# Two rows of wo loaded by the lower eight DMA engines alone, with O turned to match

## The chip, the cores and the metric

One core of one Trainium2 chip. The metric is device time of one execution in microseconds (us); each kernel ran several times, and medians, lowest and highest are quoted. The trace holds one execution of each kernel; the other executions give a time, a span (first to last instruction) and a mean granted clock only.

## The reference, cut to what matters

A decode step of attention plus an MLP, both on the normalised input, with 8 batch rows, 32 heads, 4096 keys of 128:

```python
q = (x @ wq).reshape(B, Sq, H, Dh).transpose(0, 2, 1, 3)
p = softmax(einsum("bhqd,bhkd->bhqk", q, k_cache) * Dh ** -0.5)
o = einsum("bhqk,bhkd->bhqd", p, v_cache)
A = o.transpose(0, 2, 1, 3).reshape(B, Sq, H * Dh) @ wo       # wo: 4096 x 576
h = gelu(einsum("bsd,df->bsf", layernorm(x), w1) + b1)
return x0 + A + einsum("bsf,fd->bsd", h, w2) + b2             # w2: 4608 x 576
```

The caches are 537 MB. The weights wo and w2 (10.0 MB together) are loaded last.

## The kernel before

The large operands are all streamed by SyncE's queue, in order: wq, w1, then keys and values of 32 tiles, then w2 and wo. wo is viewed as 128 partitions of 32 rows: partition `p` holds rows `32p` to `32p+31` of the matrix. A product takes one such "row" `r` of all partitions against `OT[:, r, :]`.

```python
CUTS = (0, 12, 23, 30, RO)                     # RO = 32: four loads of wo
...
sy.wait_ge(sem["kf"], NX * (NT - 1) + 2)
sy.dma_start(out=w2_sb..., in_=w2_v).then_inc(w2_in, 16)
for n, (r0, r1) in enumerate(zip(CUTS, CUTS[1:])):
    if n == 1:
        sy.wait_ge(sem["kf"], NX * (NT - 1) + 5)
    wo_in.append(nc.alloc_semaphore(f"in_wo{n}"))
    to, rows = wo_rows(r0, r1), wo_v[:, r0 * D:r1 * D]
    sy.dma_start(out=to, in_=rows).then_inc(wo_in[-1], 16)
...
# TensorE, after the last tile
te.wait_ge(w2_in, 16)
hidden_part()                                  # 36 matmuls on w2, first half
te.wait_ge(sem["on"], NT)
for b in range(B):                             # turn O: 8 matmuls into S_ps[0]
    ...
hidden_part()                                  # 36 matmuls on w2, second half
te.wait_ge(sem["on"], NT + 1)                  # VectorE has copied S_ps[0] to OT
for n, (r0, r1) in enumerate(zip(CUTS, CUTS[1:])):
    te.wait_ge(wo_in[n], 16)
    for r in range(r0, r1):                    # two matmuls a row
        ins = accumulate(te, OT[:, r, :], rows[:, r - r0, :], stop=(r == RO - 1))
```

The softmax here doesn't subtract the row's maximum and nothing guards it: scores larger than these inputs give would overflow.

## Time and profile before

| | before |
|---|---|
| time, median of the first three runs | 1292.88 us (1292.85 to 1292.97) |
| span of the traced run | 1291.5 us |
| memory stream over the span | 431 GB/s |
| w2 landed | 1277.83 us |
| TensorE's last matmul ends | 1289.56 us |

The profile's chain of waits of the kernel before; columns: start, length, what.

```profile
1248.87 4.03 PE s_ps L651 x9
...
1252.92 24.91 DMA ring<-in_B_w_dram
1277.83 0.04 issue
1277.87 4.49 PE acc L377 x36
1282.36 0.54 PE s_ps L701 x8
1282.90 6.68 PE acc L377 x100
1289.58 0.03 issue
1289.60 0.45 DVE fin L604
```

Read it from the bottom: the final cast waits for TensorE, TensorE works without a break from 1277.87 on, and what released it there is w2's load. The last loads of wo don't appear, so each had landed before TensorE asked for it.

The timeline of TensorE's matmuls in the last 18 us, kernel before; columns: start, length, engine, line, operation, result and sources, how many, and the idle time before it with its releaser.

```profile
1277.87 4.49 PE L377 MATMUL acc<-ring,hT_sb 128*8 128x288 bf16 x36 [2.77 <-DMA ring<-in_B_w_dram]
1282.29 0.61 PE L701 MATMUL s_ps<-low,Ox 128*128 128x32 bf16 x8
1282.83 2.81 PE L377 MATMUL acc<-ring,hT_sb 128*8 128x288 bf16 x36
1285.47 4.09 PE L377 MATMUL acc<-ring,OT 128*8 128x288 bf16 x64
```

The same 36 matmuls take 4.49 us the first time and 2.81 us the second: the granted clock, the share of full speed that TensorE is given, was 0.5 from 1276.94 to 1283.77 and full after it.

The trace also records sixteen landing increments for each of these loads, as many as the profile counts DMA engines; they are read here as one for each engine. Fourteen of w2's fall between 1275.99 and 1276.95, and the last two at 1277.80 and 1277.83. A 16 KB instruction packet passed at 29.99 us and another at 75.88 us (1.02 and 1.03 us). Of the later cache loads' sixteen increments, one came 1.1 us after the others from the first packet on, and two from the second on. So two engines, called the late ones here, each took one packet and stayed behind to the end.

### The profile page before, as it was taken

To read this page: it belongs to the slowest core of one execution; us is meant where nothing else is said; L and a number is where in the kernel's file an instruction comes from. 1 tells how busy PE (TensorE), PEld (TensorE's weight loads), DVE (VectorE), ACT (ScalarE), POOL (GpSimd) and SP (SyncE) were. 2 spreads that over 40 slices of the span, in tenths; PEclk is the share of its full clock that TensorE was granted. 3 is DMA by queue.
4 is the path that set the end of the run, shared out by engine and by line. 5 is a ranking of instruction groups with operands and counts; after the bars stand their busy time and mean duration, and the time that the engine had idled before them with its cause. 6 is when DMAs were issued, how large, how long until landed. Compare 5 with 4: busy or idle time off the path is not lost. (4 is left out here: it accounts for less than half of the span.)

```text
span 1291.5 us, 14664 instructions
## 1 busy us (share of the span) xinstructions
PE 734.5 (57%) x4707; PEld 321.8 (25%) x4707; DVE 829.2 (64%) x740; ACT 56.7 (4%) x181; POOL 2.4 (0%) x12
## 2 busy tenths in 40 slices
PE   4654565554565554565554565554566554565557
PEld 1222232222222222222222232222222222222223
DVE  2655677655677655677655677655677655577654
ACT  2000000000000000000000000000000000000000
POOL 0000000000000000000000000000000000000000
PEclk8778887778887777887777887778887777888778
DMA  9999999999999999999999999999999999999998
GB/s 421 440 425 436 436 426 447 426 426 449 424 426 451 422 428 449 422 430 447 422 438 438 426 436 436 426 445 428 426 447 426 426 449 424 426 451 422 430 447 348
DMA packets 10409, 557.00 MB, mean 431 GB/s; under 512 B 1163, under 2 KB 1188, under 8 KB 1446
## 3 DMA queue, kind: packets, MB, share of 16 engines
q1 hardware_dynamic: 10368, 556.93, 99.7%
q8 instruction: 2, 0.03, 0.0%
q10 hardware_dynamic: 38, 0.02, 0.0%
q14 instruction: 1, 0.01, 0.0%
HBM read 556.94 MB, written 0.01 MB: 431 GB/s over the span
## 5 line engine op out<-in xcount | busy, mean ns | idle before, releaser
L651 PE MATMUL s_ps<-ring,ident 128*128 x2048 | 541.1, 421 | 517.4 <-PEq L649 516.9
L559 DVE TENSOR_TENSOR ring<-ring,qb 128x4096 bf16<-128x4096 bf16 x256 | 578.9, 2282 | 281.8 <-DMA ring<-in_A_k_cache_dram 281.5
L651 PEld LDWEIGHTS s_ps<-ring,ident 128*128 128x128 bf16 x2048 | 216.4, 106 | 829.3 <-issue 678.7
L534 DVE TENSOR_REDUCE sc<-s_ps 128x32 f32<-128x512 f32 x256 | 171.3, 682 | 0.0
L670 PE MATMUL o_ps<-ring,ebd 128*32 128x512 bf16 x2048 | 116.4, 380 | 0.0
L546 DVE TENSOR_TENSOR ebd<-es,head 128x1536 bf16<-128x1536 bf16 x64 | 77.8, 1216 | 0.0
L569 DVE RECIPROCAL rec<-tot_ps 128x8 f32<-128x8 f32 x32 | 6.6, 207 | 110.8 <-PE oT_ps L678 110.8
L582 ACT ACTIVATE es<-sc 128x192 bf16<-128x192 f32 x64 | 19.8, 310 | 1104.2 <-DVE sc L534 1104.2
L670 PEld LDWEIGHTS o_ps<-ring,ebd 128*32 128x32 bf16 x2048 | 51.6, 97 | 62.6 <-issue 13.6
L678 PE MATMUL oT_ps<-selc,ob 128*128 128x8 f32 x256 | 33.9, 259 | 12.3 <-ACT ob L586 12.3
L678 PEld LDWEIGHTS oT_ps<-selc,ob 128*128 128x128 f32 x256 | 31.0, 191 | 15.2 <-ACT ob L586 15.2
L586 ACT ACTIVATE ob<-o_ps 128x512 f32<-128x512 f32 x32 | 19.1, 597 | 80.3 <-PE o_ps L670 80.3
L428 DVE TENSOR_SCALAR ring<-ring 96x384 f32<-96x384 f32 x2 | 0.7, 352 | 26.5 <-ACT ring L427 26.5
L545 DVE TENSOR_TENSOR Es<-Ep 128x1 f32<-128x1 f32 x32 | 5.1, 160 | 13.3 <-ACT es L582 13.3
L674 PEld LDWEIGHTS tot_ps<-headf,Es 128*128 128x128 f32 x64 | 9.5, 187 | 13.6 <-issue 13.6
L674 PE MATMUL tot_ps<-headf,Es 128*128 128x8 f32 x64 | 12.4, 266 | 0.0
L582 ACT ACTIVATION_READ_ACCUMULATOR es<-sc 128x1 f32 x64 | 11.9, 186 | 0.0
L417 PE MATMUL o_ps<-ring 128*32 128x384 bf16 x27 | 7.9, 861 | 2.9 <-DMA ring<-in_B_w_dram 2.9
L574 DVE TENSOR_TENSOR Ox<-on,quad 128x32 bf16 x32 | 6.2, 192 | 4.8
L377 PE MATMUL acc<-ring,hT_sb 128*8 128x288 bf16 x72 | 7.3, 381 | 2.8 <-DMA ring<-in_B_w_dram 2.8
L417 PE MATMUL s_ps<-ring 128*32 128x384 bf16 x27 | 7.9, 863 | 0.0
L339 PE MATMUL tot_ps<-ident,ring 40*128 40x16 bf16 x9 | 0.7, 206 | 11.6 <-DVE ring L317 11.6
(76 smaller groups left out, 61.5 us busy)
## 6 DMA issues: line engine op xcount, KB each, us to landing
ring<-in_B_w_dram SPq DMA_DIRECT2D x2, 5184.0 KB, 25.2
ring<-in_A_wq_dram SPq DMA_DIRECT2D x1, 4608.0 KB, 13.7
ring<-in_A_wo_dram SPq DMA_DIRECT2D x1, 1728.0 KB, 28.6
ring<-in_A_wo_dram SPq DMA_DIRECT2D x1, 1584.0 KB, 26.5
ring<-in_A_wo_dram SPq DMA_DIRECT2D x1, 1008.0 KB, 28.5
ring<-in_A_k_cache_dram SPq DMA_DIRECT2D x32, 31.9
ring<-in_A_v_cache_dram SPq DMA_DIRECT2D x32, 30.5
ring<-in_A_wo_dram SPq DMA_DIRECT2D x1, 288.0 KB, 28.7
```

Of the source, the lines that this page charges most:

```text
L377: i = e.matmul(acc[m][m * OP:m * OP + B, :ND], lhsT=lhsT, rhs=rhs[:, m * ND:(m + 1) * ND], start=start, stop=stop)
L417: i = e.matmul(h_ps[j][s * MP:(s + 1) * MP], lhsT=lhsT, rhs=wv[:, r0:r0 + HK, :], **flags)
L534: ins = ve.tensor_reduce(out=sc[:, n * CB:(n + 1) * CB], in_=bank_of(x).rearrange("p (c d) -> p c d", d=DL), axis=AX.X, op=ALU.add)
L546: ve.tensor_tensor(out=ebd[:, ja:jb], in0=es[:, a:b].rearrange("p (j c) -> p j c", c=4).unsqueeze(2) .to_broadcast([P, nj, G, 4]), in1=hea ...
L559: ve.tensor_tensor(out=k, in0=k, in1=qb[:, bass.ds(t, 1), :].to_broadcast([P, CB, Dh]), op=ALU.mult,).then_inc(sem["prod"], 1)
L569: ve.reciprocal(out=rec[:], in_=tot_ps[:, :G]).then_inc(sem["rec"], 1)
L582: sa.activation(out=es[:, a * CB:b * CB], in_=sc[:, a * CB:b * CB], func=ACT.Exp, scale=scale, accum_out=Ep[:, i:i + 1]).then_inc(sem["x"], 1)
L586: sa.activation(out=ob[:].rearrange("r c d -> r (c d)"), in_=o_ps, func=ACT.Copy).then_inc(sem["ob"], 1)
L651: ins = te.matmul(to, lhsT=idn, rhs=k[:, :, d * DL:(d + 1) * DL], start=(d == 0), stop=(d == Dh // DL - 1))
L670: ins = te.matmul(o_ps[m * MP:(m + 1) * MP, :], lhsT=ebd[:, j].rearrange("p g c -> p (g c)"), rhs=vals[:, c:c + 4, :], start=(j < M), stop ...
L674: te.matmul(tot_ps[:, :G], lhsT=Es[:].to_broadcast([P, P]), rhs=headf[:], start=True, stop=True).then_inc(sem["vf"], 1)
L678: ins = te.matmul(oT_ps[:, :G], lhsT=ob[:, c, :], rhs=selc[:, c, :], start=(c == 0), stop=(c == 3))
```

## The change

The intent is to take work from the two late engines. The eight engines that carry the new loads are called the lower eight here, the other eight the upper. Packet records carry no engine number; followed from packet to packet, neither late one carried a packet of the eight-row x load (eight landing increments in the trace of before). That the new loads run on the same eight engines as the x load, and so without the late ones, was the assumption; no trace had shown it. The change takes rows 0 and 1 of wo (288 KB) out of the ordinary load and has the lower eight carry them alone, in four loads of 32 partitions, whose source counts to eight in its outermost dimension. That count puts the rows on partitions in another order, so TensorE turns O's two rows to match.

```diff
-    CUTS = (0, 12, 23, 30, RO)
+    SHIFT = 2
+    CUTS = (0, SHIFT, 12, 23, 30, RO)
...
+    act(["ident"], ["turned"], lambda e: e.activation(
+        func=ACT.Copy, out=turned[:].rearrange("p (q e j) -> p q e j", e=NE, j=NJ),   # NE, NJ = 8, 4
+        in_=idn.rearrange("p (q j e) -> p q e j", e=NE, j=NJ)))
...
-        sy.dma_start(out=to, in_=rows).then_inc(wo_in[-1], 16)
+        if r1 > SHIFT:
+            sy.dma_start(out=to, in_=rows).then_inc(wo_in[-1], 16)
+            continue
+        st, w = RO * D, (r1 - r0) * D
+        for q in range(0, P, NE * NJ):
+            in_ = rows[q:q + 1]
+            sy.dma_start(
+                out=to[q:q + NE * NJ],
+                in_=bass.AP(in_.tensor, in_.offset, [[st, NE], [NE * st, NJ], [1, w]])
+            ).then_inc(wo_in[-1], 16)
...  # VectorE
     ve.wait_ge(sem["end"], 2)
+    ve.tensor_copy(
+        out=OT[:, :SHIFT], in_=S_ps[1][:, :SHIFT * B].rearrange("p (r b) -> p r b", b=B)
+    ).then_inc(sem["on"], 1)
+    ve.wait_ge(sem["end"], 3)
...  # TensorE
-    for n, (r0, r1) in enumerate(zip(CUTS, CUTS[1:])):
-        te.wait_ge(wo_in[n], 16)
+    te.matmul(
+        S_ps[1][:, :SHIFT * B], lhsT=turned[:], rhs=OT[:, :SHIFT].rearrange("p r b -> p (r b)"),
+        start=True, stop=True).then_inc(sem["end"], 1)
+    for n in (1, 0, *range(2, len(wo_in))):
+        r0, r1 = CUTS[n], CUTS[n + 1]
+        if not n:
+            te.wait_ge(sem["on"], NT + 2)
+        te.wait_ge(wo_in[n], 16 if n else 16 * P // (NE * NJ))
```

The four loads stand in the queue right behind w2 and ahead of the rest of wo.

More of the change, by code (lines that the diff above doesn't have):

```diff
@@ L181, in decode @@
     OT = sb("OT", [P, RO, B], BF16)
+    NE, NJ = 8, 4
+    turned = sb("turned", [P, P], BF16)
     hT_sb = sb("hT_sb", [P, R, 2 * B], BF16)
@@ L452, in decode @@
     mlp_done = [od.last(e) for e in ("tensor", "vector", "scalar")]
-    CUTS = (0, 12, 23, 30, RO)
+    SHIFT = 2
+    CUTS = (0, SHIFT, 12, 23, 30, RO)
+    HOMES = 12
     W2_AT = home(NT, 0)
     WO_AT = (W2_AT + 2 * R * D, home(NT - 1, 0))
-    assert WO_AT[0] + CUTS[1] * D <= WO_AT[1] and (RO - CUTS[1]) * D <= 3 * BLOCK
+    assert WO_AT[0] + HOMES * D <= WO_AT[1] and (RO - HOMES) * D <= 3 * BLOCK
     w2_sb = ring[:, W2_AT:WO_AT[0]].rearrange("p (v r d) -> p v r d", v=2, d=D)
     def wo_rows(r0, r1):
-        at = WO_AT[0] + r0 * D if r0 < CUTS[1] else WO_AT[1] + (r0 - CUTS[1]) * D
+        at = WO_AT[0] + r0 * D if r0 < HOMES else WO_AT[1] + (r0 - HOMES) * D
         return ring[:, at:at + (r1 - r0) * D]
@@ L480, in decode @@
     for n, (r0, r1) in enumerate(zip(CUTS, CUTS[1:])):
-        if n == 1:
+        if r0 == HOMES:
             sy.wait_ge(sem["kf"], NX * (NT - 1) + 5)
@@ L603, in decode @@
     ve.wait_ge(sem["end"], 2)
+    ve.tensor_copy(
+        out=OT[:, :SHIFT], in_=S_ps[1][:, :SHIFT * B].rearrange("p (r b) -> p r b", b=B)
+    ).then_inc(sem["on"], 1)
+    ve.wait_ge(sem["end"], 3)
     ve.tensor_copy(out=fin[:B], in_=acc[0][:B, :ND]).then_inc(fin_d, 1)
-    sa.wait_ge(sem["end"], 2)
+    sa.wait_ge(sem["end"], 3)
     sa.activation(
```

## The prediction

> **What bounds the kernel now.** The memory stream: the slices show a DMA share of 9 tenths nearly throughout, 431 GB/s over 1291.5 us. The change acts on the last 15 us. There the chain of waits ends: w2's load lands at 1277.83; then TensorE runs without a gap to 1289.58 (36 matmuls of the hidden part 4.49 us at half clock, 8 that turn O 0.54 us, 36 + 64 on `acc` 6.68 us); then the casts and two stores.
>
> **What is late in the stream.** The trace records sixteen landing increments for each load. After about 85 us fourteen of them fall within 1 us, the last two about 1.1 us later (last wo load: 1287.06 to 1288.00, then 1288.84 and 1288.88). By the packets, the two late ones each took one 16 KB instruction packet (at 29.99 and 75.88 us, 1.02 us each) and never caught up. Neither carried packets of the eight-row x load[...].
>
> **What the change moves.** wo's rows 0 and 1 are 288 KB, 18 KB per engine. The upper eight lose 18 KB: 0.68 us at the 27.2 GB/s of a 64 KB packet (2.41 us). The lower eight gain sixteen 2,304-byte packets of 94 ns and have eight packets shortened: +0.83 us (estimate). So the last landing should come at 1288.4 to 1288.6 instead of 1288.88, set now by the lower engines.
>
> **How much is critical.** Next to nothing. In the wo part TensorE takes 61.3 ns per `acc` matmul (starts 122.5 ns apart per row) and shows no gap. Row 12 starts at 1286.94, its load landed at 1285.75; row 23 at 1288.29, landed 1288.17; row 30 at 1289.15, landed 1288.88. Every load is there, by 0.12 us at the closest. What starts TensorE is w2, issued ahead of the shifted rows; its landing stays at 1277.8.
>
> **What the change adds.** On TensorE's critical run: one 128x128 weight load and a matmul of 16 columns. The eight like it took 67 ns each at half clock, plus about 0.14 us to change over; at full clock I estimate 0.05 to 0.15 us. VectorE's copy of the turned rows (0.2 to 0.4 us) hides behind the 20 matmuls of rows 2 to 11 (1.2 us). Three more issues on SP come 20 us ahead of need; the extra ScalarE copy falls in an idle stretch before 17.7 us.
>
> **Prediction.** Before 1292.88; after 1292.95 us, 8 in 10 between 1292.5 and 1293.4. Faster by over 2%: 0.005; within 2%: 0.99; slower by over 2%: 0.005.
>
> **What would show it.** Right: w2 still lands near 1277.8; the last landing is 0.3 to 0.5 us earlier, and no two engines stand 1.1 us behind in the last wo loads; TensorE runs gapless from w2 to its end, near 1289.65. Wrong: gaps in the wo part; TensorE waiting for rows 0 and 1; the new loads on sixteen engines.
>
> **What would make it wrong.** The granted clock returns to full at 1283.77; it may do so elsewhere in unprofiled runs, and with a faster TensorE the last landing would bind, giving back up to 0.4 us. The added instructions may move an instruction packet to another time or engine, which moves w2's landing by up to 1.1 us either way.

The sum is 1292.88 us plus the turn, estimated at 0.05 to 0.15 us.

## More of the kernel before

Sums over three stretches of the kernel before (a packet is counted where it starts, so a DMA share can pass 1); columns: stretch, its length, busy time of PE, PEld, DVE, ACT, POOL, granted clock, DMA share, GB/s.

```profile
core 0: us, PE busy (x) PEld busy (x) DVE busy (x) ACT busy (x) POOL busy (x), PEclk, DMA share, GB/s
1275.60:1276.80 1.20, 0.00 (x0) 0.00 (x0) 0.19 (x1) 0.00 (x0) 0.00 (x0) 1.00 1.02 432
1276.80:1278.20 1.40, 0.33 (x4) 0.23 (x6) 0.00 (x0) 0.00 (x0) 0.00 (x0) 0.55 0.98 415
1278.20:1280.00 1.80, 1.80 (x20) 0.94 (x16) 0.00 (x0) 0.00 (x0) 0.00 (x0) 0.50 0.99 419
```

The stream is even here.

## The result, and the profile after

| | before | after |
|---|---|---|
| time, median of 6 runs | 1292.86 us (1292.79 to 1292.97) | 1294.28 us (1293.27 to 1295.38) |
| time and span of the traced run | 1293.01, 1291.5 us | 1293.60, 1292.0 us |
| w2 landed, last two engines | 1277.80, 1277.83 us | 1278.52, 1278.73 us |
| w2 landed, the other fourteen | 1275.99 to 1276.95 us | 1276.02 to 1276.61 us |
| last landing of wo | 1288.88 us | 1289.09 us |
| clock returns to full | 1283.77 us | 1283.17 us |

The ratio of the times is 1.0011 (95% interval 0.9998 to 1.0024). Ratios here are the mean time of one kernel's fast runs over that of the other's of the same rounds, so not quite the ratio of the medians quoted. The median lies 1.4 us above and the runs spread over 2.1 us instead of 0.2.

The rows did move: of the ordinary load of rows 2 to 11, six engines landed at 1280.25 to 1280.85 and ten at 1281.80 to 1282.20, as fits six upper engines with less to carry, eight lower ones with more, and the two late ones. In the last load of wo, too, no two engines stand apart any more.

The chain of waits after the change:

```profile
1252.86 25.87 DMA ring<-in_B_w_dram
1278.73 0.04 issue
1278.78 4.49 PE acc L383 x36
1283.26 0.34 PE s_ps L725 x8
1283.60 2.30 PE acc L383 x36
1285.90 0.12 PE s_ps L732
1286.02 4.04 PE acc L383 x64
1290.05 0.02 issue
```

It has the same form, with the turn (L732) added. What moved is its head: w2's load takes 25.87 us instead of 24.91, though nothing stands ahead of it in the queue that did not before.

TensorE's timeline after the change:

```profile
1278.78 4.49 PE L383 MATMUL acc<-ring,hT_sb 128*8 128x288 bf16 x36 [3.49 <-DMA ring<-in_B_w_dram]
1283.19 0.41 PE L725 MATMUL s_ps<-low,Ox 128*128 128x32 bf16 x8
1283.53 2.37 PE L383 MATMUL acc<-ring,hT_sb 128*8 128x288 bf16 x36
1285.84 0.18 PE L732 MATMUL s_ps<-OT,turned 128*128 128x16 bf16 x1
1285.95 4.09 PE L383 MATMUL acc<-ring,OT 128*8 128x288 bf16 x64
```

The same stretches after the change:

```profile
1275.60:1276.80 1.20, 0.00 (x0) 0.00 (x0) 0.32 (x2) 0.00 (x0) 0.00 (x0) 0.81 1.05 388
1276.80:1278.20 1.40, 0.00 (x0) 0.00 (x0) 0.00 (x0) 0.00 (x0) 0.00 (x0) 0.50 1.08 258
1278.20:1280.00 1.80, 1.23 (x12) 0.69 (x14) 0.00 (x0) 0.00 (x0) 0.00 (x0) 0.50 0.94 393
```

This is the finding. For 1.4 us the engines are as busy as ever (share 1.08) but move 258 GB/s instead of 415. The packet records say how: at first the packets of the new loads, 2,304 bytes each, take 93 to 100 ns; from 1276.9 on they take some 185 ns, and the ordinary ones slow with them, those of 11,520 bytes from 436 to some 830 ns and the last w2 packets of the two late engines from 773 to 1147 and 1380 ns. After 1278.5 all is normal again. So the late engines, the very ones to be relieved, are held up while they finish w2. Of the 0.90 us by which w2's last landing moved, 0.61 are in the last packet itself, 0.18 in its later start and 0.11 between its end and the landing. Below, a packet of 2,304 bytes is called slow when it took over 140 ns, and the time with slow packets the slow phase. Here 34 packets were slow, though the third and fourth new load have 64: what decides when the slow phase sets in is not shown.

### The profile page after: what moved, and what is told of

Read it like the earlier page. It is cut to its first block, busy times and chain, and to the rows that moved or that the text cites. A ratio compares the mean times of both kernels' runs of the same rounds, so it can differ in the third digit from the quotient of the medians.

```text
span 1292.0 us, 14672 instructions
## 1 busy us (share of the span) xinstructions
PE 733.0 (57%) x4708; PEld 321.3 (25%) x4708; DVE 829.6 (64%) x741; ACT 56.9 (4%) x182; POOL 2.4 (0%) x12
```

## The experiments

Two theories and their rivals were put on record. **P**: the loads for partitions 64 to 127, the third and fourth new load, are the harm; new loads for this half are called crossing below. That they do harm only while the upper engines are busy was the guess, which no trace had shown; the last experiment tests it. **M**: the memory side is slowed by short reads of many rows. **C**: the times vary because the return of the granted clock falls differently in each run. The 3.41 us that C uses are measured: in the traces of before and after, each stretch of one granted clock between two changes lasts a multiple of 3.41 us (6.83 to 27.31 us).

### The changed kernel again

> The changed kernel, unaltered. Theory P[...]: two of the four new loads write to partitions 64 to 127[...]; all packets then take about twice as long (185 instead of 93 ns for 2,304 bytes) for 1.5 us, and the two late engines, still on w2, land w2 0.7 to 0.9 us later. Theory C (clock, for the spread): times fall into two groups, near 1293.3 and near 1295.0, 1.7 us apart, which is half of one 3.41 us window of the granted clock; a run in the upper group has TensorE at half clock for one more window after w2 lands. Rival R: the spread is noise, and the times fill the range 1293.3 to 1295.4 evenly.

Measured: 1293.40, 1293.67, 1293.68, 1295.21, 1295.72 us, ratio 1.001; before on the same chip 1292.77 to 1294.34. The trace repeats the slow phase (40 slow packets of 2,304 bytes, 1276.85 to 1278.19) and w2's late landing (1278.53). Times near 1293.5 and near 1295.5 came again; the reason given for the two groups is taken up below.

### The two halves in the other order

```diff
-        for q in range(0, P, NE * NJ):
+        for q in (64, 96, 0, 32):
```

> The same four loads, but those for partitions 64 to 127 issued first. Theory P: the slow phase moves to the first two loads (about 180 ns a packet from 1275.7 us on), the last two run at 93 to 100 ns, and the w2 landings of the fourteen early engines are late too; w2's last landing stays at or above 1278.3. Rival M (memory side: short reads of many rows slow the stream whenever both halves are on wo): the slow phase stays with the third and fourth load, from 1276.8 us on, as in the changed kernel.

Measured: median 1293.52 us (1293.37 to 1295.80), ratio 1.0008. Two stretches of its sums:

```profile
1275.60:1276.80 1.20, 0.00 (x0) 0.00 (x0) 0.18 (x1) 0.00 (x0) 0.00 (x0) 0.82 0.97 250
1276.80:1278.20 1.40, 0.00 (x0) 0.00 (x0) 0.00 (x0) 0.00 (x0) 0.00 (x0) 0.50 1.00 260
```

The slow phase starts some 0.8 us earlier, at 1276.16 (250 instead of 388 GB/s in the first stretch), and the fourteen early engines now land w2 as late as 1277.77 (1276.61 in the change), the last at 1278.61. The onset follows the destination, as P expects, and not the place in the sequence. But packets stay slow to 1278.1, when loads for partitions 0 to 63 were expected to run freely, and 91 of them are slow instead of 34; engines reach the second pair at different times, and this run does not sort that out.

### The turn alone

Rows 0 and 1 come in one ordinary load; TensorE turns by an identity.

```diff
-        in_=idn.rearrange("p (q j e) -> p q e j", e=NE, j=NJ)))
+        in_=idn))                                # and out=turned[:] unrearranged
...
-        if r1 > SHIFT:
+        if True:
...
-        te.wait_ge(wo_in[n], 16 if n else 16 * P // (NE * NJ))
+        te.wait_ge(wo_in[n], 16)
```

> Rows 0 and 1 in one ordinary load over 128 partitions and sixteen engines; TensorE still turns O, by an identity. This is the TensorE part of the change alone. Both theories P and M: no slow phase, w2 lands at 1277.8, TensorE's run is 0.12 us longer, the time is 1292.9 to 1293.1, spread as small as before's. If the turning itself costs more than the trace shows, 1293.3 or above.

Measured: median 1293.26 us (1292.84 to 1294.34), ratio 1.0003. No slow packet, w2 at 1277.88, spans 1291.4 to 1291.8. The turn does not bring the slow phase. The stretch that was slow in the change:

```profile
1276.80:1278.20 1.40, 0.27 (x4) 0.17 (x6) 0.00 (x0) 0.00 (x0) 0.00 (x0) 0.50 1.01 421
```

In this trace the clock was full again at 1282.64, 1.1 us earlier than in the trace of before, and the chain of waits ends with the landing of rows 23 to 29 (1288.30) and not with w2's. So with before's loads, too, it depends on the clock which load sets the end.

The times spread more than expected although the spans don't: two runs have 2.1 and 2.7 us between span and time, where 1.3 to 1.6 is usual. These two runs were not traced, so what passes there, after the last instruction or before the first, was not seen.

### The same reads, written to partitions 0 to 63

The third and fourth load go to a second tensor on partitions 0 to 63; TensorE takes rows 0 and 1 as four products over 64 partitions. The result stays right.

```diff
+    second = sb("second", [HP, 2 * D], BF16)     # HP = 64
...
-                out=to[q:q + NE * NJ],
+                out=to[q:q + NE * NJ] if q < HP else second[q - HP:q - HP + NE * NJ, :],
...
+        if not n:
+            for h in range(2):
+                at = second[:] if h else wo_rows(r0, r1)[:HP]
+                for r in range(SHIFT):
+                    accumulate(te, OT2[:, h, r, :], at[:, r * D:(r + 1) * D])
+            continue
```

> The loads read the same rows on the same eight engines in the same order, but the third and fourth write to partitions 0 to 63 of another tensor; TensorE takes rows 0 and 1 as four products of 64 partitions (right result, 4 matmuls and one turn more, about 0.3 us). Theory P: no slow phase, packets at 93 to 100 ns throughout, w2's last landing back at 1277.8, time 1293.2 to 1293.4 with a small spread. Rival M: the reads are the same, so the slow phase stays, w2 lands at 1278.5 to 1278.8, and the time is 1293.6 to 1295.6.

Measured: median 1293.17 us (1292.61 to 1293.77), ratio 1.0001. The stretch that was slow:

```profile
1276.80:1278.20 1.40, 0.47 (x8) 0.36 (x10) 0.00 (x0) 0.00 (x0) 0.00 (x0) 1.00 1.09 448
```

No packet of 2,304 bytes took over 140 ns, w2 landed at 1277.69, rows 23 to 29 at 1287.99, the last of wo at 1288.65. The reads, their order and the engines are those of the change, so M falls. That the new tensor is not what helps is shown by the mirror below, which has one too. It was run again later:

> The version that keeps to partitions 0 to 63 once more, for its spread. Theory P: packets at 93 to 100 ns, w2 at 1277.7; spans of 1291.2 to 1292.4 with no run near 1293.5, times 1292.6 to 1293.8; if the upper group of the changed kernel does not come from the crossing loads, about two runs in five have spans of 1293 or more.

Measured: 1292.67, 1292.95, 1292.97, 1293.84, 1293.85 us; spans 1291.2 to 1292.5; no slow packet; w2 at 1277.97. As expected.

### The mirror: all four loads to partitions 64 to 127

```diff
-                out=to[q:q + NE * NJ] if q < HP else second[q - HP:q - HP + NE * NJ, :],
+                out=to[q:q + NE * NJ] if q >= HP else second[q + HP:q + HP + NE * NJ, :],
```

(and the products on partitions 64 to 127)

> The mirror of the version that keeps to partitions 0 to 63: all four new loads write to partitions 64 to 127 (right result, same reads, same matmuls as that version). Theory P: the slow phase starts with the first load at 1275.7 us and lasts about twice as long, 16 packets per lower engine at some 185 ns, 3 us; w2's last landing 1278.9 to 1279.4; rows 23 to 29 land at about 1289.1; lowest time 1293.9 to 1294.3. Rival M: as the changed kernel, w2 at 1278.5 to 1278.7, lowest time 1293.3 to 1293.6.

Measured: median 1295.34 us (1294.84 to 1297.09), ratio 1.002 (1.0006 to 1.0034).

```profile
1275.60:1276.80 1.20, 0.00 (x0) 0.00 (x0) 0.19 (x1) 0.00 (x0) 0.00 (x0) 1.00 1.01 265
1276.80:1278.20 1.40, 0.00 (x0) 0.00 (x0) 0.00 (x0) 0.00 (x0) 0.00 (x0) 0.99 1.06 219
1278.20:1280.00 1.80, 0.72 (x8) 0.40 (x10) 0.00 (x0) 0.00 (x0) 0.00 (x0) 0.50 0.95 317
```

This is the dose: none of the loads crossing, 0 slow packets; two of four, 32 to 45 in the order of the change (91 in the other order); all four, 97. w2's last landing grows with it in both orders: 1277.7 to 1278.0, 1278.4 to 1279.0, and 1279.24; rows 23 to 29 landed at 1289.12, as expected. From 1276.8 to 1278.2 the stream moved 219 GB/s, where it moved 448 with none crossing. The lowest time is 0.5 us above what was expected.

### Eight neighbouring partitions a load

Sixteen loads of eight partitions in their natural order, with an identity for the turn.

```diff
+        for q in range(0, P, NE):
+            sy.dma_start(out=to[q:q + NE], in_=rows[q:q + NE]).then_inc(wo_in[-1], 16)
```

> Rows 0 and 1 in sixteen loads of eight neighbouring partitions each, in their natural order[...]; TensorE turns O by an identity. [...] Rival H (only which half of the partitions matters): loads to 0 to 63 run at 94 ns, the others at about 185, and the time is that of the changed kernel.

Measured: median 1294.49 us (1294.07 to 1296.22), ratio 1.0013. From 1276.2 on, 54 packets were slow, most of them 150 to 190 ns, the slowest 316; w2 landed at 1279.15, and one engine landed rows 23 to 29 at 1289.87. Neither expectation holds. The first, now cut, was a time of 1295 to 1298 us; it rested on a grouping of partitions that no trace or run of this case shows. Against H, five packets begun by 1276.25 were slow (148 to 202 ns): the first of these packets began at 1275.72, so no engine had yet come to its ninth (at 93 ns or more a packet, 0.53 us is time for six at most; the count is one packet of each load for each of eight engines), and all five went to partitions 0 to 63. The half is thus not the whole condition, and it stays open what this arrangement runs into.

### The clock

Ten idle matmuls (thirteen in the changed kernel) before the wait for w2, so that TensorE is not idle when it lands:

```diff
+    for _ in range(10):
+        te.matmul(S_ps[2], lhsT=idn, rhs=qb[:, 0:4, :].rearrange("p t d -> p (t d)"), start=True, stop=True)
     te.wait_ge(w2_in, 16)
     hidden_part()
```

> The kernel before with ten idle matmuls of 512 columns between the last tile and the wait for w2, so that TensorE does not stand idle and its granted clock is still full when w2 lands. Theory C (the clock at w2's landing sets TensorE's end): TensorE then runs ahead of the loads and its end is set by the last loads, wo rows 23 to 31: landing 1288.17 plus 18 matmuls, 1.3 us; time 1292.8 to 1292.9. If TensorE falls back to half clock while it waits for the wo loads, the last 18 matmuls take 2.2 us instead and the time is 1293.6 to 1294.4.

Measured: median 1293.66 us (1293.18 to 1293.80), ratio 1.0005. The mechanism is as expected: the clock is 1.0 until after TensorE's last matmul (both blocks of 36 matmuls take 2.37 us), and TensorE now waits for wo (18 matmuls after rows 23 to 29 land at 1288.33). The time is not: it is 0.3 us or more above, and three of the runs have 2.1 us outside the span, where 1.3 to 1.6 is usual.

> The changed kernel with thirteen such matmuls. Theory C with theory P: no upper group near 1295; w2 still lands at 1278.5 to 1278.8 and the lower eight engines still land rows 23 to 29 last, at 1288.4, so the time is 1293.2 to 1293.3 in nearly all runs. If the upper group comes from something else than the clock at w2's landing (loads that stall longer, or a clock that falls at the very end), runs near 1295 remain.

Measured: 1292.95, 1293.22, 1293.25, 1294.55, 1294.94 us, ratio 1.0008. Its timeline:

```profile
1278.47 2.37 PE L383 MATMUL acc<-ring,hT_sb 128*8 128x288 bf16 x36 [0.71 <-DMA ring<-in_B_w_dram]
...
1286.06 1.51 PE L383 MATMUL acc<-ring,OT 128*8 128x288 bf16 x22 [0.90 <-DMA ring<-in_A_wo_dram]
1288.50 1.27 PE L383 MATMUL acc<-ring,OT 128*8 128x288 bf16 x18 [0.92 <-DMA ring<-in_A_wo_dram]
```

With the clock full, w2's delay no longer reaches the end; rows 23 to 29, which landed at 1288.45, set it. But two runs of five still lie above 1294.5 (spans 1293.2 and 1293.6). They were not traced, so that their clock was full as well is likely but not shown; if it was, theory C does not explain the upper group.

> The version whose new loads keep to partitions 0 to 63, with ten such matmuls. Theories P and C: w2 at 1277.7, rows 23 to 29 landed at 1288.0, time 1292.5 to 1292.7 in nearly all runs, which would beat before by 0.2 to 0.3 us.

Measured: 1292.27, 1292.58, 1292.67, 1293.54, 1294.63 us against 1292.71 to 1293.26 for before: a median 0.24 us lower, but a ratio of 1.0002 (0.9989 to 1.0016). Three runs lie within the expected range or below it, two above, one of them with a span of 1293.3. No version is shown to beat before.

### More looks at the changed kernel

> The changed kernel once more, for a second look at a profile: about two runs in five have been near 1295. If this one is, theory C expects more than 5.9 us at half clock after w2 lands; the rival expects w2's landing itself 1.5 us later than in the first profile (1278.7).

Measured: 1292.94 us, as fast as before, with w2 landed at 1278.63. In this run the clock had fallen only at 1278.49 and was back at 1281.90:

```profile
1278.80:1282.00 3.20, 3.20 (x30) 1.71 (x28) 0.00 (x0) 0.00 (x0) 0.00 (x0) 0.52 1.02 429
1282.00:1284.40 2.40, 2.40 (x44) 1.63 (x42) 0.42 (x1) 0.00 (x0) 0.00 (x0) 1.00 1.01 427
```

> The changed kernel beside it on the same chip. Theory P: w2 at 1278.5 to 1278.8, packets at 185 ns in the third and fourth load, lowest time 1292.9 to 1293.4, and about two spans in five of 1293 or more.

Measured: 1293.25, 1293.85, 1294.27, 1295.16, 1296.62 us, ratio 1.0013. The traced run took 1294.27 us: 45 slow packets, w2 at 1278.97, full clock only from 1284.70.

> The changed kernel, one look. If the time is 1294.9 or more: theory P expects w2's landing at 1279.5 or later (a longer stall), theory C half clock until 1286 or later; in an ordinary run w2 lands at 1278.4 to 1279.0 and the time follows from the return of the clock, about half a microsecond per microsecond that it returns later.

> The changed kernel, one look, with what the run before it expects: w2 at 1278.4 to 1279.0 and an end set by the return of the clock, or a longer stall or later clock if it falls in the upper group.

> The changed kernel, one look, with what the two runs before it expect: w2 at 1278.4 to 1279.0 and an end set by the return of the clock, or a longer stall or later clock if it falls in the upper group.

Measured: 1293.24, 1293.31 and 1294.74 us; w2 at 1278.76, 1278.81 and 1278.58; full clock from 1281.39, 1282.35 and 1284.47. The same two stretches in the slowest of them, where the clock was at half through both:

```profile
1278.80:1282.00 3.20, 3.20 (x30) 1.77 (x28) 0.00 (x0) 0.00 (x0) 0.00 (x0) 0.50 1.01 429
1282.00:1284.40 2.40, 2.40 (x26) 1.28 (x24) 0.43 (x1) 0.00 (x0) 0.00 (x0) 0.50 0.99 422
```

In this run 2.3 us lie outside the span of 1292.5 us. Its trace alone has a 16 KB instruction packet that begins after the last instruction (at 1293.84, 1.13 us); whether the one comes from the other is not shown.

These traces settle how the clock works in. Count TensorE's end as its start after w2, plus half of the time that it then spent at half clock, plus a remainder. The half fits because the same 36 matmuls take 4.49 us at half clock and 2.37 us at full. The remainder is 8.74 us before, and 8.95 us in each of the three traces of the changed kernel in which TensorE alone sets the end and the clock came late (half clock for 5.72, 5.68 and 5.85 us after its start). The difference, 0.21 us, is the turn; the two versions with the clock kept full agree (from the start of the second 36 matmuls to the first on wo 2.21 us before, 2.42 us after). In the first trace of the changed kernel the remainder is 9.06, and what the other 0.11 us are is open. The three earliest returns (1281.39 to 1282.35) give 9.35 to 9.84: there TensorE waits for wo instead. The clock's stretches near the end lasted 3.41, 6.83 or 10.24 us, so it changes on a grid of 3.41 us, and the place of this grid against the kernel's start differed from trace to trace.

### The new loads behind all others

```diff
-    for n, (r0, r1) in enumerate(zip(CUTS, CUTS[1:])):
+    for n in (*range(1, len(wo_in)), 0):         # on SyncE, and the same order on TensorE
```

> The changed kernel with its four new loads issued after all the others, and rows 0 and 1 multiplied last. Theory P: by then the early upper engines are done, so at most a dozen of the packets of 2,304 bytes in the new loads are slow, w2 lands at 1277.8, rows 2 to 31 have landed by 1288.3, rows 0 and 1 by about 1288.9; spans 1291.2 to 1292.2, times 1292.6 to 1293.5, no run at 1294.9 or more. If the upper group comes from issuing or counting loads on eight engines as such, it stays: two runs in five at 1294.9 or more.

Measured: 1292.94, 1293.00, 1293.11, 1293.91, 1294.04 us, ratio 1.0004; before on that chip 1292.63 to 1293.14. w2 landed at 1278.07, without a slow packet, and no run reached 1294.9, as expected. Two runs (1293.91 and 1294.04) lie above the expected 1293.5. Another miss is the count of slow packets, 31 instead of a dozen. At 1287.7 us ten packets were under way, all of 2,304 bytes, and all ten were slow (168 to 191 ns):

```profile
1287.50:1288.00 0.50, 0.50 (x10) 0.20 (x6) 0.00 (x0) 0.00 (x0) 0.00 (x0) 1.00 0.47 92
```

By 1287.26 fourteen engines had landed all the other loads, so the ten are the eight of the new loads and the two late ones. The crossing thus costs time even where six of the eight upper engines are idle, and at 92 GB/s, under half of the 219 of the mirror. The guess that it takes busy upper engines is thus not enough: with two of the eight busy, all ten packets were slow.

## Why the prediction was wrong

- **Right: what bounds the end.** w2's landing starts TensorE, which then runs without a gap; landing wo earlier alone would gain nothing. The chain after the change has that form. It does so only where the clock returns late: in five traces with a return at 1281.39 to 1282.70 (the turn alone, the new loads behind all others, and three of the changed kernel) the chain ends with rows of wo instead.
- **Wrong, and the step that failed: "What starts TensorE is w2, issued ahead of the shifted rows; its landing stays at 1277.8."** Its place ahead in the queue did not protect w2: packets of other engines' new loads ran beside its last packets and these slowed. w2's last landing went to 1278.73 (1278.5 to 1279.0 in all traces of the changed kernel) and came back to 1277.7 to 1278.0 when of the loads only the destination partitions were changed. That the destination half is the cause is shown by none, two and four crossing loads; how crossing slows the packets is not. The prediction asked which engines the new loads use, and not which partitions they write to.
- **Wrong: the last landing at 1288.4 to 1288.6.** It was 1289.09, later than before. The sum nearly held where nothing crossed (1288.60, 1288.65 and 1288.76); the missing term is the slow phase.
- **Too small: the turn, 0.05 to 0.15 us.** The traces give 0.21.
- **Half right: the clock.** It was named as something that might give back up to 0.4 us, in one direction alone. With w2's landing, and with the wait for wo where it returns early, it sets TensorE's end: 1289.64 to 1290.81 in the seven traced runs, which took 1292.94 to 1294.74 us.
- **The sum for the traced run.** w2 starts TensorE 0.91 us later; 4.40 instead of 5.90 us at half clock takes back 0.75; the remainder grows by 0.32, of which the turn is 0.21. Together that is the 0.48 us by which TensorE's end moved (1289.56 to 1290.04). The sum closes because the remainder is what is left over; its test is the other traces, of which three have 8.95 us, 0.11 below this one.
- **Open: the upper group.** Seven of twenty runs of the changed kernel took 1294.9 us or more, against none of 42 of before, 10 of the version on partitions 0 to 63, 5 of the turn alone and 5 with the new loads last. So it goes with the crossing loads while w2 is on its way. The border is not sharp: the other thirteen reach 1294.27 and 1294.74, so rival R, an even spread, is not excluded; and by the span, single runs without crossing loads came near it (one of before with 1293.0, one of the warmed version on partitions 0 to 63 with 1293.3, against 1293.5 to 1295.3 in the group). None of the seven traced runs fell into it, so what is later in such a run has not been seen. The first six runs' median, 1.4 us above before's, lies between three runs of the low group (1293.27 to 1293.60) and three of the upper one (1294.96 to 1295.38): without the upper group the rise would have been some 0.4 us.

## What to carry to other kernels

Before bytes are moved to less loaded DMA engines, look at which partitions these engines will write to; here the same loads were harmless on partitions 0 to 63 (448 GB/s from 1276.8 to 1278.2 us) and halved the stream's rate on 64 to 127 (219 GB/s). When a queue is rearranged, check every load in flight at that moment, not just those behind the change, and first of all the one that the critical engine waits for. A difference of half a microsecond at the end of a kernel needs the clock's phase read from each trace before it is put down to anything: with its return at 1281.39 to 1284.70 us, TensorE's end lay at 1289.64 to 1290.81 in the seven traces of the changed kernel. The 16 KB instruction packets took 1.02 to 1.09 us in the traces of before and after, and in that of before the two late engines were still 1.1 us behind nearly 1200 us after the second. Issues took different times too: in the trace after the change the four loads with a two-step source took 0.67 to 0.82 us each on SyncE's queue, ordinary ones 0.33 to 0.45; the sixteen loads of eight partitions took mostly 0.27 to 0.30 in their run. Here it was off the critical path.
